# First batch of an attention and two-layer kernel: one pair of heads gets its own query and key buffers, six attention units move ahead in the planner's list, two move back

## Chip, cores and metric

The kernel runs on one core of one Trainium2 chip. The metric is the device time of one execution in microseconds, the median of the runs shown.

## What is computed

The reference, cut to what matters here: attention over 4 batches of 8 heads (576 positions, head size 64), where the first four heads see the last 32 positions and the other four see positions at multiples of 32, then two layers over the 2304 tokens.

```python
scores = scale * np.matmul(q, k.transpose(0, 1, 3, 2))
mask_local = (rel >= 0) & (rel < stride)
mask_strided = (rel >= 0) & (pos[None, :] % stride == pos[:, None] % stride)
scores = np.where(masks[None, :, :, :], scores, -1000000000.0)
scores = scores - np.max(scores, axis=-1, keepdims=True)
attn = np.exp(scores)
attn = attn / (np.sum(attn, axis=-1, keepdims=True) + 1e-09)
x = np.matmul(attn, v)            # per token: 8 heads x 64 = 512 values
h = np.maximum(np.maximum(x @ w1, x @ w2), x @ w3)     # 512 -> 768
x = h @ w_out                                          # 768 -> 512
h = x @ w_in                                           # 512 -> 2048
g = np.maximum(h, 0.0) + alpha * np.minimum(h, 0.0)
out = g @ w_out                                        # 2048 -> 512
```

All of it is float32. Dense products are made of three matmuls each, on a high and a low part of both factors (the pairs high-high, high-low, low-high).

## The kernel before

**The front of the kernel is list-scheduled.** The class `Weave` holds tasks: engines that may run one, a cost, a function that emits its instructions, a place in a list (`pos`), the events that it needs and gives, and the ring buffers that it takes and uses. When the program is built, `plan` goes through them: of all tasks whose needs are met and whose buffers will come free, it lets each engine take what can start first. Among tasks of an engine that can start within 120 ns of the earliest, the smallest `pos` goes first. A task off PE that reads a PSUM bank gets `pos - 1000`, so banks are emptied first. Buffers of the rings "q", "v", "e", "pt", "x" and "word" are handed out in the order in which the tasks were added. Each engine then runs its instructions in the order so planned.

**Attention.** Each batch has eight units, taken in the order of `ATT_UNITS`: heads in four pairs `cc`, two parts `hf` each. `(2, 0), (2, 1), (3, 0), (3, 1)` are the strided pairs, `(0, 0), (1, 0), (0, 1), (1, 1)` the local ones, whose `hf` is the half of the tokens. So the first six units of a batch give all that the first half of its tokens needs, and units seven and eight complete the second half. A unit is: scores on PE (L317), mask and row minimum on DVE (L325), exponentials on ACT (L332), reciprocals (L343, L344) and normalisation on DVE or ACT (L356, L354), transposes on PE (L367), copies of these to SBUF (L256), products with the values on PE (L392), then a high part of the output by a cast (L256) and a low part by a subtraction (L259). Two units of batch 0 have filler matmuls ahead of their first or second transposes (`UNREAD`, L362: three in unit three, nine in unit six), whose results nobody reads.

The tasks of batch 0 have `first, last = -32, -8` and `step = 2.4`: unit i (from 0) stands at -32 + 2.4 i, its transposes 2.4 later, its values 4.8 later. A pair's loads (L287 and L289 for queries and keys, L294 for values, all issued by SP) stand 8 places ahead of its first unit. Queries and keys have two buffers each (`qkp`), values two, exponentials three.

**Weights of the first layer.** 24 tiles (18 "gate", 6 "mix") come as float64 words: SP loads one (L437, three buffers `raw`), ACT rebases it (L451), DVE joins its words (L455, L457), ACT or DVE makes the high part (L256), DVE the low part (L259). Tile n stands at 1.5 n - 12 in the list, its load 4.5 earlier.

**Dense products.** One product of the first layer (L580, 12 matmuls of 128x288) needs one gate tile and the four pairs' outputs of one half of the tokens. They stand in the list from 0 on, in the order of `GATES_FIRST`: output features 0 and 1 of the first half, then feature 0 of the second half, then alternating. Three weights make one feature, of which the maximum is taken (L667, L670). L602 is the layer's second product. Attention of batch 1 stands from place 16 on, and its tasks run between the dense products.

**Later weights.** From place 44 on, the second layer's weights are converted as well and written to DRAM from three store tiles (`wst`, L489). What follows the list (the last batch's products, then the second layer, L986 to L1185) is written in a fixed order.

```python
weave = Weave({"bank": 8, "q": 2, "v": 2, "e": 3, "pt": 4, "x": 11, "t": 4, "h": 12,
               "raw": 3, "word": 6, "wst": 3})
...
add(load(592), emit_qk, pos, gives=[qk], makes=[("q", qk)])
...
first, last = (-32, -8) if b == 0 else ((b - 1) * NUNITS + (16 if b == 1 else 3), b * NUNITS - 3)
step = (last - first) / (len(ATT_UNITS) + 2)
...
attention_tasks(b, cc, hf, first + step * i, step)
```

## Time and profile before

| | us |
|---|---|
| median of 3 runs | 751.76 |
| lowest and highest run | 750.66, 752.38 |
| profiled execution, first to last instruction (span) | 747.7 |
| PE busy in it | 732.9 |
| PE weight loads (PEld) busy | 710.3 |
| DVE busy | 640.3 |
| ACT busy | 464.5 |

The profile gives the span of the profiled execution and not its device time; the device times are those of the runs, whose median lies 4.1 us above the span. "Idle before" in a row is the time in which the engine stood still just ahead of an instruction, with what ended it. PE is matmuls, PEld the weight loads, which run beside them. Matmuls are pipelined, so the rows of successive groups overlap a little. SPq is the queue of SP, from which all transfers here are issued. [...]

### The profile page before, as it was taken

What the parts mean: (1) busy time and instruction counts of PE and PEld (TensorE: products, weight loads), DVE (VectorE), ACT (ScalarE), POOL (GpSimd) and SP (SyncE); (2) the same over time, 40 slices, a digit from 0 to 9 for tenths busy, and PEclk for the clock granted to TensorE, in tenths of its full rate; (3) what the DMA queues carried; (4) which work ended last, traced back from release to release, by engine and by line L of the source; (5) the groups of instructions that cost most, each with busy time, mean ns of one, the idle gap of its engine ahead of it and who ended that gap; (6) DMA issues with size and microseconds to landing.
All of it is one profiled execution on the core that took longest, in us unless ns stands there. A gap on an engine that the chain in (4) does not pass through costs nothing.

```text
span 747.7 us, 16003 instructions
## 1 busy us (share of the span) xinstructions
PE 732.9 (98%) x5560; PEld 710.3 (95%) x5560; DVE 640.3 (86%) x1711; ACT 464.5 (62%) x1254; POOL 28.7 (4%) x42
## 2 busy tenths in 40 slices
PE   5899999999999999999999999999999999999998
PEld 4699999999999999999999999999999999999997
DVE  4899999899898999478868898888989888988896
ACT  5987889568684788423345666634666654556571
POOL 1000000000000000023500000000000000000000
PEclk9999999999999999999999999999999999999999
DMA  7477769996999765779899789999789999867362
GB/s 248 155 244 227 234 206 337 342 342 244 323 318 340 252 219 208 253 267 332 306 319 400 266 293 332 383 401 372 265 286 316 364 401 369 289 236 254 118 201 77
DMA packets 88929, 211.96 MB, mean 283 GB/s; under 512 B 11024, under 2 KB 41232, under 8 KB 88848
## 3 DMA queue, kind: packets, MB, share of 16 engines
q1 hardware_dynamic: 88848, 210.94, 80.4%
q8 instruction: 44, 0.72, 0.4%
q14 instruction: 37, 0.30, 0.1%
HBM read 154.80 MB, written 56.10 MB: 282 GB/s over the span
## 4 chain that ended last, share of the span: by engine, by line
PE 94%; ACT 2%; DMA 2%; DVE 1%; issue 0%; SPq 0%; ACTq 0%; DVEq 0%
PE bank L580 24%; PE ph L1185 23%; PE po L986 15%; PE bank L602 10%; PE bank L753 4%; PE po L992 4%; PE ph L986 3%; PE bank L317 3%; PE bank L392 2%; PE bank L367 2%; PE po L996 2%; ACT e L332 1%; DMA wh<-w 1%; DMA k<-in_kTs 0%; PE po L1185 0%; DMA wo<-w 0%
## 5 line engine op out<-in xcount | busy, mean ns | idle before, releaser
L1185 PE MATMUL ph<-x,w 128*128 128x384 f32 x990 | 200.1, 337 | 0.0
L580 PE MATMUL bank<-x,w 128*128 128x288 f32 x1440 | 197.5, 296 | 0.0
L580 PEld LDWEIGHTS bank<-x,w 128*128 128x128 f32 x1440 | 191.8, 188 | 2.1
L1185 PEld LDWEIGHTS ph<-x,w 128*128 128x128 f32 x990 | 166.3, 188 | 1.0
L986 PE MATMUL po<-w,g 128*128 128x256 f32 x936 | 135.6, 281 | 0.0
L986 PEld LDWEIGHTS po<-w,g 128*128 128x128 f32 x936 | 130.1, 189 | 0.4
L1191 DVE TENSOR_TENSOR c<-ph,c 128x384 f32<-128x384 f32 x165 | 89.5, 555 | 30.5 <-PE ph L1185 27.4
L979 ACT CAST g<-c 128x384 fp32r<-128x384 f32 x93 | 47.0, 505 | 91.1 <-DVE c L1169 51.7
L602 PE MATMUL bank<-h,w 128*128 128x288 f32 x576 | 79.4, 297 | 0.0
L602 PEld LDWEIGHTS bank<-h,w 128*128 128x128 f32 x576 | 76.9, 188 | 0.9
L256 ACT CAST w<-word 128x512 fp32r<-128x512 f32 x100 | 58.0, 590 | 24.8 <-DMA wh<-w 7.9
L332 ACT ACTIVATE e<-e,nm 96x128 f32<-96x128 f32 (+2 forms) x176 | 68.1, 396 | 6.1 <-DVE nm L325 5.9
L259 DVE TENSOR_TENSOR w<-word,w 128x512 fp32r<-128x512 f32 x100 | 63.4, 642 | 9.2 <-ACT w L256 8.9
L1129 ACT ACTIVATE c<-c 128x384 f32<-128x384 f32 x96 | 50.5, 526 | 32.9 <-DVE c L1191 31.8
L1130 ACT ACTIVATE c<-c,nalpha 128x384 f32<-128x384 f32 x96 | 59.2, 617 | 3.1
L1134 DVE SCALAR_TENSOR_TENSOR c<-c 128x384 f32<-128x384 f32 x96 | 53.1, 553 | 6.1 <-ACT c L1130 6.1
L980 DVE TENSOR_TENSOR g<-c,g 128x384 fp32r<-128x384 f32 x96 | 53.0, 552 | 0.9 <-ACT g L979 0.5
L451 ACT ACTIVATE word<-raw 128x512 f32<-128x512 f32 x56 | 37.6, 682 | 14.6 <-DMA raw<-in_w 10.8
L980 DVE TENSOR_TENSOR g<-k,g 128x384 fp32r<-128x384 f32 x72 | 37.2, 558 | 7.5 <-ACT g L979 7.5
L992 PE MATMUL po<-w,g 128*128 128x512 f32 x120 | 43.0, 397 | 0.0
L457 DVE SCALAR_TENSOR_TENSOR word<-raw,word 128x512 uint32<-128x512 uint32 x56 | 38.8, 692 | 1.9
L1169 DVE TENSOR_TENSOR k<-c 128x384 f32<-128x384 f32 x72 | 37.9, 551 | 0.0
(107 smaller groups left out, 939.1 us busy)
## 6 DMA issues: line engine op xcount, KB each, us to landing
w<-wh SPq DMA_DIRECT2D x72, 512.0 KB, 5.3
raw<-in_w SPq DMA_DIRECT2D x50, 512.0 KB, 5.1
w<-wo SPq DMA_DIRECT2D x48, 512.0 KB, 5.8
w<-wp SPq DMA_DIRECT2D x36, 512.0 KB, 6.4
wh<-w SPq DMA_DIRECT2D x24, 512.0 KB, 5.0
xd<-xst SPq DMA_DIRECT2D x28, 384.0 KB, 3.2
x<-xd SPq DMA_DIRECT2D x28, 384.0 KB, 8.2
ws<-w SPq DMA_DIRECT2D x12, 512.0 KB, 5.4
```

The lines of the kernel that those rows point to most:

```text
L256: (nc.scalar.copy if e == "ACT" else nc.vector.tensor_copy)(out_, in_)
L259: nc.vector.tensor_tensor(out=out_, in0=x, in1=y, op=ALU.subtract)
L332: nc.scalar.activation(tl[ek][:nq, j, i, :nk], tl[ek][:nq, j, i, :nk], AF.Exp, bias=tl["nm", u][:nq, j, i:i + 1], scale=-1.0, accum_out=tl ...
L580: nc.tensor.matmul(acc, words["gate", f, g][:, wi, cc * P:(cc + 1) * P], xt[b, cc, hf][:, xi, :], start=n == 0, stop=n == 3 * NCC - 1)
L602: nc.tensor.matmul(acc, words["mix", f][:, wi, dc * P:(dc + 1) * P], st["h", hf, f][:, xi, :], start=n == 0, stop=n == 3 * NF1 - 1)
L980: return g, lambda: nc.vector.tensor_tensor(out=g[:, 1], in0=x, in1=g[:, 0].bitcast(F32), op=ALU.subtract)
L986: nc.tensor.matmul(bank[:, NH * half:NH * (half + 1)], g[:, gi, t * P:(t + 1) * P], w[:, wi, off:off + NH], start=first and i == 0, stop=l ...
L992: nc.tensor.matmul(bank.rearrange("p (s n) -> p s n", n=NH), g[:, 0, t * P:(t + 1) * P], w[:, :, off:off + NH], start=first, stop=last)
L1130: nc.scalar.activation(a, a, AF.Copy, scale=nalpha[:, f:f + 1])
L1134: nc.vector.scalar_tensor_tensor(out=a, in0=h, scalar=0.0, in1=a, op0=ALU.max, op1=ALU.add)
L1185: nc.tensor.matmul(bank, words["h", n, i][:, wi, off + c * P:off + (c + 1) * P], x2h[blk, k, c][:, xi, :], start=m == 0, stop=m == 5)
L1191: nc.vector.tensor_tensor(out=out_, in0=bank, in1=other, op=ALU.add)
```

## The change

The third pair of heads of batch 0 (`cc = 0`, units five and seven) takes its queries and keys from a pool of its own, which lies in memory where the store tiles come later; the store tiles' pool is opened when the first of them is asked for, after the front pool is closed. In the list, units one to six of batch 0 move 200 places ahead, with transposes 0.3 and values 0.6 places behind their unit's first tasks; units seven and eight move ten places back (from -17.6 and -15.2 to -7.6 and -5.2), with the same 0.3. The places of all loads, of the weights, of the dense products and of the other batches stay.

```diff
+FRONT_POS, FRONT_STEP = -200, 0.3
...
-    qkp = pool(ax, "qkp", 2)
+    qk_pool = pool(ax, "qkp", 2)
...
-    wst = pool(conv_x, "wst", 3, "right")
+    front_x = ExitStack()
+    front_qk = pool(front_x, "fqk", 1, "right")
...
-    weave = Weave({"bank": 8, "q": 2, "v": 2, "e": 3, "pt": 4, "x": 11, "t": 4, "h": 12,
+    weave = Weave({"bank": 8, "q": 2, "third q": 1, "v": 2, "e": 3, "pt": 4, "x": 11, "t": 4, "h": 12,
                    "raw": 3, "word": 6, "wst": 3})
...
+        third = (b, cc) == (0, 0)
+
         def emit_qk(_):
+            qkp = front_qk if third else qk_pool
             q = qkp.tile([P, S], F32, tag="q", name="q")
...
-        add(load(592), emit_qk, pos, gives=[qk], makes=[("q", qk)])
+        add(load(592), emit_qk, pos, gives=[qk], makes=[("third q" if third else "q", qk)])
...
+    stores = []
+
+    def store_tile():
+
+        if not stores:
+            front_x.close()
+            stores.append(pool(conv_x, "wst", 3, "right"))
+        return stores[0].tile([P, 2, DM], F32R, tag="w", name="w")
...
-                    lambda: wst.tile([P, 2, DM], F32R, tag="w", name="w"), pos,
+                    store_tile, pos,
                     makes=[("wst", sk)], given=given)
...
-            attention_tasks(b, cc, hf, first + step * i, step)
+            attention_tasks(b, cc, hf, first + step * i + (FRONT_POS if i < 6 else 10) * (b == 0),
+                            step if b else FRONT_STEP)
```

## Rows read from the trace of the kernel before

**Rows 1.** The page's first part: busy us (share of span), instructions.

```profile
PE 732.9 (98%) x5560; PEld 710.3 (95%) x5560; DVE 640.3 (86%) x1711; ACT 464.5 (62%) x1254; POOL 28.7 (4%) x42
```

**Rows 2.** Busy us by stretch: us, length, engines, granted clock, DMA share, GB/s.

```profile
20.00:40.00 20.00, 17.41 (x187) 13.59 (x188) 18.09 (x103) 20.00 (x88) 0.00 (x0) 1.00 0.55 174
40.00:60.00 20.00, 20.00 (x153) 19.96 (x152) 19.36 (x43) 16.73 (x49) 0.00 (x0) 1.00 0.74 238
```

**Rows 3.** PE's waits: total us, times, longest; second row is from 38 to 300 us.

```profile
PE bank L317 <- DMA k<-in_kTs: 5.9, 2, 4.5
...
PE bank L317 <- ACT pt L256: 0.3, 1, 0.3
```

**Rows 4.** PE's timeline, 16 to 71 us: start, us, line, tiles, count, idle before.

```profile
16.50 1.32 PE L317 MATMUL bank<-k,q 64*96 64x128 f32 x12
...
20.70 0.90 PE L317 MATMUL bank<-k,q 64*96 64x128 f32 x12
...
26.20 0.72 PE L392 MATMUL bank<-pt,v 128*64 128x96 f32 x12 [0.41 <-ACT pt L256]
26.84 2.34 PE L362 MATMUL bank<-ident_r 128*128 128x512 f32 x9
29.79 1.00 PE L367 MATMUL bank<-ident,e 96*128 96x96 f32 x6 [0.61 <-DVE e L356]
...
33.11 0.71 PE L367 MATMUL bank<-ident,e 96*128 96x96 f32 x6
...
35.39 0.47 PE L367 MATMUL bank<-ident,e 96*128 96x96 f32 x3
...
36.81 0.82 PE L317 MATMUL bank<-k,q 64*108 64x108 f32 x12
37.56 0.95 PE L392 MATMUL bank<-pt,v 128*64 128x96 f32 x12
38.45 32.11 PE L580 MATMUL bank<-x,w 128*128 128x288 f32 x240
```

**Rows 5.** The timeline of ACT and DVE, 21 to 38 us.

```profile
21.87 1.23 ACT L451 ACTIVATE word<-raw 128x512 f32<-128x512 f32 x2
...
26.81 0.41 ACT L332 ACTIVATE e<-e,nm 96x128 f32<-96x128 f32 x1
...
28.56 0.16 DVE L343 TENSOR_SCALAR rc<-sm 96x6 f32<-96x6 f32 x1
...
30.43 0.38 DVE L455 TENSOR_SCALAR word<-word 128x512 uint32<-128x512 uint32 x1
...
30.84 0.69 DVE L457 SCALAR_TENSOR_TENSOR word<-raw,word 128x512 uint32<-128x512 uint32 x1
...
31.73 0.69 ACT L256 COPY pt<-bank 128x288 f32<-128x288 f32 x2
...
33.69 0.41 ACT L256 CAST x<-bank 128x288 fp32r<-128x288 f32 x1
...
34.14 0.46 DVE L259 TENSOR_TENSOR x<-bank,x 128x288 fp32r<-128x288 f32 x1 [0.70 <-ACT x L256]
...
36.70 0.68 DVE L259 TENSOR_TENSOR w<-word,w 128x512 fp32r<-128x512 f32 x1
```

**Rows 6.** Weight tiles finished on DVE, 0 to 72 us: ns min/median/max, first and last start.

```profile
L259 DVE TENSOR_TENSOR w<-word,w x15: 681/684/694, 36.7 to 71.7; 128x512 fp32r<-128x512 f32 x15
```

**Rows 7.** SP's queue, 7 to 15 us; key loads to landing; first and last store.

```profile
7.25 0.43 SPq L289 DMA_DIRECT2D k<-in_kTl  x1
7.72 1.38 SPq L437 DMA_DIRECT2D raw<-in_w  x3
14.70 0.43 SPq L289 DMA_DIRECT2D k<-in_kTl  x1
...
k<-in_kTl SPq DMA_DIRECT2D x8, 304.0 KB, 4.9
...
L489 SPq DMA_DIRECT2D wh<-w x32: 319/382/1348, 105.6 to 198.5; - x32
```

## The prediction

> **What bounds the kernel now.** I read the page's busy shares first. PE is busy 732.9 of 747.7 us [rows 1], so the only time to be won is time in which PE idles or waits. The table by stretches says where that is: in 20 to 40 us PE is busy 17.41 of 20.00 and its weight loads only 13.59, from 40 us on both are full [rows 2]. The list of PE's waits says the same: 5.9 us for the first key loads, and from 38 us to 300 us a single wait of 0.3 us [rows 3]. So everything hangs on when the stream of dense products begins, and on how much PE work is then already done. PE's timeline gives that start: 38.45 us, 240 matmuls in a row without a gap [rows 4].

> What ended last before it is read from the chain of waits and the rows of ACT and DVE. ACT is busy 20.00 of 20.00 in 20 to 40 us [rows 2]: it is the bound of the front. The first dense product (first half of the tokens, first weight) needs the attention output of the first six units of batch 0 and one finished weight tile. The sixth unit's output is finished by the subtraction at 34.14, thus at 34.60; the first weight tile by the subtraction at 36.70, thus at 37.38; then PE still has scores of batch 1 (36.81) and the eighth unit's values (37.56) ahead of it in its queue [rows 4, 5]. Units seven and eight, which this product doesn't need, sit in between: their twelve exponentials begin at 26.81 and hold the copies of the sixth unit's transposes back to 31.73, though those transposes start at 29.79 [rows 4, 5].

> **The change, part by part.** Four edits, told as three.

> *Own buffers for the third pair.* Its query and key loads no longer wait for the first pair's buffers; before the keys were issued at 7.25. A key load lands 4.9 us after its issue (median), so about 12.2, and the unit's scores run at 16.50: 4 us of slack. The fourth pair's keys, issued at 14.70, now take the first pair's buffers; they landed by about 19.6 and their scores run at 20.70, behind other PE work: 1 us of slack [rows 4, 7]. What really holds these scores is the ring of three exponential buffers, which is not touched. Behind them in SP's queue the first three weight loads move: past one more pair of some 0.6 MB, about 3 us at the pace at which weight tiles of 512 KB come later (2.5 us each). They were issued from 7.72, so their data would be there by about 21 instead of 18, as three follow each other; the first is read at 21.87 and joined at 30.43 [rows 5 to 7]. Bounds: nothing gained, 1 us lost if that cover went; taken: 0, since the first reader is nearest to the first of the three. The store tiles, made only once the front's buffers are closed, are first sent at 105.6, long after the last score of batch 0: 0 [rows 7].

> *First six units ahead, transposes and values right behind their unit (0.3 places instead of 2.4).* These units already stood ahead of the weights, and an instruction that empties a bank goes first anyway. So I expect the first 26 us as before, 0 from the order alone, within 1 us either way (the size of the waits in this stretch, PE idle before the sixth unit's transposes 0.61) [rows 4].

> *Units seven and eight ten places later.* The three weight tiles of the first output feature (places -12, -10.5, -9) now stand ahead of them (-7.6, -5.2), and so does the sixth unit's tail. On ACT the twelve exponentials from 26.81 to 31.73 (4.9 us) leave the path, as do the mask steps on DVE that push the sixth unit's reciprocal to 28.56 [rows 5]. What is late next: the nine filler matmuls ahead of the sixth unit's first transposes, from 26.84 for 2.34 us, to 29.18 [rows 4]. Transposes then start at 29.2 (before 29.79), are done about 30.0; the copies take 0.69 for two, 30.7; the values 0.72, 31.4; the cast 0.41 and the subtraction 0.46, **32.3**. The weight tile: joined on DVE at 30.43 before, in 1.1 us, and finished at 37.38 because its subtraction waited until 36.70. With the weights ahead, join 1.1, cast and subtraction (0.68, as much taken for the cast) follow each other: 30.4 + 2.4 = 32.8 at the latest, about 31 if the join moves ahead with the reciprocal [rows 5]. So the dense stream starts at about **32.5**, 5.95 us earlier. Bounds: 32.0 (nothing but the fillers and the tail) and 38.45 (as before).

> Against that, PE's work that stood between 33 and 38.45 must still be done inside the stream: transposes of units seven and eight 0.71 + 2 x 0.47, their values 2 x 0.72 (the row at 26.20; that at 37.56 includes waiting), two groups of scores of batch 1, 0.82 each at most. That is 4.73, less some 0.07 overlap at each of seven seams (36.81 + 0.82 ends after 37.56): **4.2 us** [rows 4]. Net -5.95 + 4.2 = -1.75. After that PE must not starve. A weight tile is finished every 2.5 us (fifteen from 36.7 to 71.7) and feeds one product of 12 matmuls, 1.6 us (32.11 / 20), while only the first half of the tokens is there, 3.2 us once both are [rows 4, 6]. The gap of 0.9 us per tile is covered by the 4.2 us of pushed-back work for four to five tiles, some 11 us. Taken: no idle.

> [...]

> **Sum.** On the profiled execution: 747.7 - 1.75 = 745.95 of span. The median of the runs is 4.1 above that span (751.76 - 747.7), kept as it is: 751.76 - 1.75 = **750.0 us**. About 0.2%, 1.5 us, is what a measurement of this kernel can tell from no change, so the forecast lies just beyond it.

> **Rivals.**

> A larger gain. If the planner also fills PE's remaining holes before the start (the 0.61 before the transposes, the stretched value rows, most of the 2.34 of fillers), 2 to 3 us more go: 747.5. For it: PEld only 13.59 of 20.00 [rows 2]. Against: ACT is full all through. 0.12.

> No gain: the list is only a preference. Each engine takes what can start first, so the idle PE may run units seven and eight's scores where it did, their mask steps go ahead as bank-emptiers, and the dense stream starts where the weights allow. A start at 36.5 would win 1.95 and pay about 2 back: 751.6. For it: the first weight tile was as late as the attention [rows 5]. 0.20.

> Slower: the second half comes too late. Now the weights stand ahead of units seven and eight on ACT and DVE, both full [rows 2]. Place: the dense stream after 32.5. Price: 0.9 us of PE idle per tile that serves only one half, less the 4.2 us of filling work and the gain of 1.75. It turns into a loss where the second half is later than 5.95 / 0.9 = 6.6 tiles (about 49 us); at eight tiles, 52.5 us, it is 7.2 - 4.2 - 1.75 = +1.25, at nine +2.15: 753.0 to 753.9, taken at 753.5. For it: DVE needs 2.5 us per tile with little else to do [rows 6]. Against: only the first three tiles outrank unit seven, the fourth and fifth unit eight. 0.20 (with later waits of a newly ordered list in it).

> The clock falls. If PE is slow again at the start of the stream, matmuls cost 1.32 / 0.90 there. The trace has PE slow from the first scores (4.5) to past 16.50, 12 us at most [rows 3, 4]; in a full stream I take half, 6 us, of which 1 - 0.90 / 1.32 = 0.32 is lost: -1.75 + 1.9 = 751.9, the loss bounded by 0 and 3.8. [...] 0.06.

> **How the numbers follow.** The forecast keeps 0.42, of which 0.08 falls short of 1.5 us. Faster: 0.34 + 0.12 = 0.46. Same: 0.08 + 0.20 + 0.06 = 0.34. Slower: 0.20. The forecast's own range is 748.9 to 751.0 (start at 32.0 to 33.5). The range for eight in ten takes in most of the larger gain and of the loss: 746.8 to 753.9.

> **What would show it.** Right: the first dense matmul between 32 and 33.5, with fewer than 240 matmuls in its first unbroken run; the transposes, values and batch 1's scores inside it; the copies of the sixth unit's transposes directly behind them; PE waits after the start below 0.5 us. Wrong: the first dense matmul past 36; PE waits on weight subtractions or on the second half's outputs after it; dense matmuls spaced above 0.134 us in the first microseconds; new waits past 100 us.

## The result, and the profile after

The changed kernel takes **759.49 us** (median; 758.33 to 763.68 in four runs) against 751.22 for the kernel before on the same chip: ratio 1.0122 as estimated from the runs (it is not the quotient of the medians), 95% interval 1.0097 to 1.0147. It is 8.3 us slower, where 750.0 was forecast and 753.9 was the upper end of the range. Lines of the code moved by two to fifteen: scores are now L322, masks L330, exponentials L337, reciprocals L348 and L349, normalisation L361 and L359, fillers L367, transposes L372, values L397, copies and casts L258, subtractions L261, weight joins L460 and L462, dense products L594. In the variants below they can lie some lines further on.

The profiled execution has a span of 756.5 us, 8.8 more than before. PE's busy time grew by 4.6 us although it runs the same 5560 matmuls [rows 1]; so it also ran slower:

```profile
PE 737.5 (97%) x5560; PEld 714.8 (94%) x5560; DVE 639.9 (85%) x1707; ACT 465.1 (61%) x1255; POOL 28.4 (4%) x42
```

In the list of PE's waits (total us, times, longest) the first of these lines stood at 1.9 us in the kernel before, and the other two are new [rows 3]:

```profile
PE bank L372 <- DVE e L361: 4.8, 2, 2.5
PE bank L594 <- ACT w L258: 3.3, 1, 3.3
PE ph L1200 <- ACT xo L823: 0.9, 1, 0.9
```

PE's timeline shows where they lie (start, us, shape and count, idle before with its releaser) [rows 4]:

```profile
19.52 0.90 PE L322 MATMUL bank<-k,q 64*96 64x128 f32 x12
20.35 0.78 PE L397 MATMUL bank<-pt,v 108*64 108x108 f32 x12
23.67 1.99 PE L372 MATMUL bank<-ident,e 126*126 126x126 f32 x10 [2.55 <-DVE e L361]
...
29.32 3.11 PE L367 MATMUL bank<-ident_r 128*128 128x512 f32 x9
...
32.62 0.90 PE L322 MATMUL bank<-k,q 64*96 64x128 f32 x12
...
38.66 6.37 PE L594 MATMUL bank<-x,w 128*128 128x288 f32 x24 [3.35 <-ACT w L258]
...
53.23 25.43 PE L594 MATMUL bank<-x,w 128*128 128x288 f32 x190 [0.56 <-DVE w L261]
78.50 1.15 PE L372 MATMUL bank<-ident,e 108*108 108x108 f32 x10
...
343.03 33.76 PE L767 MATMUL bank<-x,w 128*128 128x288 f32 x252
...
397.87 1.33 PE L1200 MATMUL ph<-x,w 128*128 128x384 f32 x6 [0.92 <-ACT xo L823]
```

Four things are to be seen. The sixth unit's scores come 1.2 us earlier than before (19.52, before 20.70). PE then stands still for 2.55 us ahead of the fourth unit's transposes. The nine fillers take 3.11 us instead of 2.34. And the dense stream starts at 38.66, no earlier than before, after another pause of 3.35 us, with 24 matmuls in 6.37 us: 0.265 us each, against 0.134 in the stream of before. Batch 1's first transposes, after 240 dense matmuls, stand at 78.50; before, the same point was 38.45 + 32.11, about 70.4. I use it below as the **checkpoint**: 8.1 us of the loss are there already. The last two rows are the longest dense run of the first layer (343.03; before it began at 335.28, so 7.75 us of the 8.8 are left there) and the start of the second layer, where 0.92 us of waiting are new.

The slow matmuls go with a lower granted clock of TensorE, the column ahead of the last two in the table by stretches (its second column is PE's busy time); in the kernel before it reads 1.00 over the whole span (0 to 748 us) [rows 2]:

```profile
22.00:24.00 2.00, 0.33 (x2) 0.23 (x3) 1.93 (x11) 2.00 (x12) 0.00 (x0) 1.00 0.00 0
24.00:26.00 2.00, 2.00 (x13) 1.51 (x14) 1.88 (x6) 2.00 (x8) 0.00 (x0) 0.55 0.00 0
26.00:28.00 2.00, 2.00 (x20) 1.56 (x16) 1.10 (x4) 1.63 (x6) 0.00 (x0) 0.50 0.14 34
...
36.00:38.00 2.00, 0.00 (x0) 0.00 (x0) 1.97 (x10) 2.00 (x12) 0.00 (x0) 0.96 0.33 126
38.00:40.00 2.00, 1.30 (x4) 0.95 (x5) 1.93 (x5) 2.00 (x9) 0.00 (x0) 0.50 0.69 205
```

Behind the first pause the clock reads 0.55 and then 0.50, and PE is busy for 2.00 of 2.00 us in each of these stretches. Behind the second it reads 0.50 from 38 to 44 us, where the 24 matmuls take their 0.265 us each.

What made the first pause is read from DVE's timeline (the first row is the end of the fourth unit's exponentials on ACT):

```profile
17.94 0.19 ACT L337 ACTIVATION_READ_ACCUMULATOR e<-e,nm 126x1 f32 x1
...
19.63 0.50 DVE L258 COPY pt<-bank 108x324 f32<-108x324 f32 x1 [1.06 <-PE bank L372]
...
20.85 0.28 DVE L330 CUSTOM_DVE_ANT_0 e<-bank,mask_l 96x128 f32<-96x128 f32 x1
...
22.59 0.16 DVE L348 TENSOR_SCALAR rc<-sm 126x4 f32<-126x4 f32 x1
...
23.15 1.64 DVE L361 TENSOR_TENSOR e<-e,rc 126x252 f32<-126x252 f32 x4
...
33.55 0.29 DVE L330 CUSTOM_DVE_ANT_0 e<-bank,mask_l 96x128 f32<-96x128 f32 x1 [3.22 <-PE bank L322]
...
36.32 0.42 DVE L460 TENSOR_SCALAR word<-word 128x512 uint32<-128x512 uint32 x1
```

and from the same rows of the kernel before:

```profile
20.15 0.16 DVE L343 TENSOR_SCALAR rc<-sm 126x4 f32<-126x4 f32 x1
...
20.55 0.75 DVE L356 TENSOR_TENSOR e<-e,rc 126x252 f32<-126x252 f32 x2
...
22.00 0.25 DVE L325 CUSTOM_DVE_ANT_0 e<-bank,mask_l 96x128 f32<-96x128 f32 x1
```

Before, the fourth unit's reciprocal (20.15) and normalisation (20.55) were done when the sixth unit's masks began (22.00). Now the six masks begin at 20.85 and stand **ahead** of that reciprocal (22.59) and normalisation (23.15), for which PE waits. The masks read PSUM banks, so the planner puts them 1000 places ahead of what empties no bank. They are not the whole of the delay: the fourth unit's exponentials were done by 18.13, and ahead of its reciprocal stood also 1.06 us in which DVE waited for PE's transposes, a copy, subtractions, and the last masks of the fifth unit. The six masks, from 20.85 to about 22.11, are 1.3 us of the 2.44 by which the reciprocal came later than before.

The second pause has its cause further down the same queue. ACT had rebased the weight words by 27.7, but DVE joins them only at 36.32: ahead of the joins stand the masks of the eighth unit (33.55, after 3.22 us of waiting for PE) and of batch 1's first unit. The eighth unit's scores (32.62) stand in PE's queue behind the nine fillers (29.32) and the first of the sixth unit's transposes.

### The profile page after: what moved, and what is told of

It is laid out like the page before. It is cut to its first block, busy times and chain, and to the rows that moved or that the text cites. A ratio compares the mean times of both kernels' runs of the same rounds, so it can differ in the third digit from the quotient of the medians.

```text
span 756.5 us, 16005 instructions
## 1 busy us (share of the span) xinstructions
PE 737.5 (97%) x5560; PEld 714.8 (94%) x5560; DVE 639.9 (85%) x1707; ACT 465.1 (61%) x1255; POOL 28.4 (4%) x42
## 4 chain that ended last, share of the span: by engine, by line
PE 74%; DVE 9%; DMA 8%; issue 3%; ACT 3%; POOL 2%; SPq 1%; POOLq 0%; ACTq 0%; DVEq 0%
PE ph L1200 23%; PE bank L594 16%; PE po L1001 15%; PE bank L616 6%; PE po L1007 4%; PE ph L1001 3%; DMA wh<-w 2%; PE bank L322 2%; PE po L1011 2%; PE bank L397 2%; PE bank L372 2%; ACT e L337 1%; DVE w L261 1%; POOL xst L215 1%; DVE e L330 1%
## 5 line engine op out<-in xcount | busy, mean ns | idle before, releaser
L594 PE MATMUL bank<-x,w 128*128 128x288 f32 x1440 | 201.8, 299 | 4.2 <-ACT w L258 3.3
L594 PEld LDWEIGHTS bank<-x,w 128*128 128x128 f32 x1440 | 194.6, 191 | 7.1 <-ACT w L258 3.5
L258 ACT CAST w<-word 128x512 fp32r<-128x512 f32 x100 | 57.6, 587 | 26.1 <-DMA wh<-w 11.5
L337 ACT ACTIVATE e<-e,nm 96x128 f32<-96x128 f32 (+2 forms) x176 | 67.8, 392 | 9.2 <-DVE nm L330 9.1
L261 DVE TENSOR_TENSOR w<-word,w 128x512 fp32r<-128x512 f32 x100 | 62.7, 640 | 9.8 <-ACT w L258 9.6
L462 DVE SCALAR_TENSOR_TENSOR word<-raw,word 128x512 uint32<-128x512 uint32 x56 | 38.8, 692 | 1.9
```

What stands on the lines that cost most here:

```text
L258: (nc.scalar.copy if e == "ACT" else nc.vector.tensor_copy)(out_, in_)
L261: nc.vector.tensor_tensor(out=out_, in0=x, in1=y, op=ALU.subtract)
L337: nc.scalar.activation(tl[ek][:nq, j, i, :nk], tl[ek][:nq, j, i, :nk], AF.Exp, bias=tl["nm", u][:nq, j, i:i + 1], scale=-1.0, accum_out=tl ...
L594: nc.tensor.matmul(acc, words["gate", f, g][:, wi, cc * P:(cc + 1) * P], xt[b, cc, hf][:, xi, :], start=n == 0, stop=n == 3 * NCC - 1)
```

## The experiments

"Clock" is the granted clock, "checkpoint" the start of batch 1's first transposes where 240 dense matmuls stand ahead of it as in the kernel before. A dash marks another order. Each ratio is to the kernel before on the same chip (medians there 750.66 to 751.22).

| variant | median us | ratio to before (95%) | longest PE pause at 21 to 28 | first dense | checkpoint |
|---|---|---|---|---|---|
| before | 751.22 | | 0.41 | 38.45 | 70.4 |
| changed | 759.49 | 1.0122 (1.0097, 1.0147) | 2.55 | 38.66 | 78.50 |
| bufs_alone | 750.95 | 0.9995 (0.9978, 1.0012) | 0.41 | 38.48 | 70.47 |
| list_alone | 752.74 | 1.0028 (1.0010, 1.0046) | 2.02 | 33.46 | 71.21 |
| old_step | 751.68 | 1.0026 (1.0006, 1.0045) | 0.41 | 32.95 | - |
| no_plus10 | 756.67 | 1.0085 (1.0068, 1.0102) | 2.55 | 43.20 | 75.41 |
| no_nine | 758.19 | 1.0093 (1.0066, 1.0120) | 2.55 | 35.16 | 75.07 |
| nine_at_fourth | 755.33 | 1.0068 (1.0052, 1.0083) | 0.19 | 34.35 | 72.98 |
| nine_at_both | 758.74 | 1.0092 (1.0063, 1.0120) | 0.19 | 36.17 | 75.71 |
| bridge | 756.60 | 1.0076 (1.0059, 1.0093) | 0.19 | 34.49 | 72.20 |
| calm_sixth | 751.72 | 1.0007 (0.9996, 1.0018) | 0.97 | 33.56 | 71.97 |
| reordered | 761.57 | 1.0154 (1.0119, 1.0188) | 1.67 | 40.44 | 80.08 |
| late_fourth | 758.00 | 1.0091 (1.0065, 1.0117) | 1.99 | 41.80 | 73.71 |
| nine_and_calm | 752.81 | 1.0028 (1.0015, 1.0040) | 0.17 | 30.80 | - |
| old_step_calm | 762.76 | 1.0158 (1.0131, 1.0184) | 0.41 | 36.35 | - |
| calm_sixth_eighth_b1 | 756.15 | 1.0091 (1.0054, 1.0127) | 0.97 | 31.81 | - |
| calm_sixth_b1 | 762.03 | 1.0145 (1.0119, 1.0171) | 0.97 | 33.89 | - |

### Which of the edits

**bufs_alone** keeps the own buffers and takes the list back.

```diff
-            attention_tasks(b, cc, hf, first + step * i + (FRONT_POS if i < 6 else 10) * (b == 0),
-                            step if b else FRONT_STEP)
+            attention_tasks(b, cc, hf, first + step * i,
+                            step)
```

> Edit: the own query and key buffers of the third pair alone, with the units at their old places and the old step in the list. Theory (the buffers cost and gain nothing by themselves, they only let the list's new places take effect): TensorE has no pause over 1 us up to 60 us, the first dense matmul is within 0.5 us of the 38.45 us of the kernel before, median 750.2 to 751.5. Rival (the earlier loads of the third pair push the first weights back, which costs): first dense matmul later by over 0.5 us, 752 or more.

Measured 750.95, no change, with the front of the kernel before. The buffers by themselves cost nothing.

**list_alone** is the opposite: the list without own buffers.

```diff
-        third = (b, cc) == (0, 0)
+        third = False
```

> The changed kernel without the third pair's own buffers: queries and keys share two buffers again, the list stays changed. Theory A (the buffers let scores, mask steps and normalisations pile up in another order, PE pauses 2.55 us at 21.1 and the granted clock falls): no pause over 1 us between 18 and 30 us, granted clock 1.00 in 24 to 32 us, first dense matmul 33 to 36, time 750 to 753. Theory B (the list places are at fault, whatever the buffers): pause and half clock as in the changed kernel, 757 to 760.

Measured +0.28% (interval 0.10 to 0.46). PE's timeline has a pause of nearly the same length, after which the clock read 0.50 in 24 to 26 us, and yet the dense stream starts five microseconds earlier than before:

```profile
23.18 1.22 PE L372 MATMUL bank<-ident,e 126*126 126x126 f32 x4 [2.02 <-ACT e L359]
...
27.74 0.90 PE L322 MATMUL bank<-k,q 64*96 64x128 f32 x12
...
33.46 2.27 PE L594 MATMUL bank<-x,w 128*128 128x288 f32 x14
```

So a pause need not be dear. Neither expectation holds as a whole: the time and the first dense matmul are theory A's, the pause and the low clock theory B's. The pause is also not the one of the changed kernel. DVE and ACT show it:

```profile
19.33 0.16 DVE L348 TENSOR_SCALAR rc<-sm 126x4 f32<-126x4 f32 x1
...
22.72 0.70 ACT L359 ACTIVATE e<-e,rc 126x126 f32<-126x126 f32 x2
```

Here the fourth unit's reciprocal (19.33) runs ahead of the sixth unit's masks (whose scores begin at 19.56), and it is the normalisation, left to ACT behind the fifth unit's exponentials, that comes late. What differs further is what stands behind the pause: the eighth unit's scores (27.74) come ahead of fillers and sixth transposes, and DVE never stands still for them.

**old_step** takes the transposes' distance back to 2.4 places, and keeps all else.

```diff
-                            step if b else FRONT_STEP)
+                            step)
```

> The changed kernel with transposes 2.4 and values 4.8 places behind their unit, as before, instead of 0.3 and 0.6. If the depth-first order makes the pause at 21.1 (theory C): transposes of the fourth and fifth unit apart again, granted clock 1.00 in 24 to 32 us, 750 to 753. If the buffers alone make it (theory A): pause and clock as in the changed kernel, 757 to 760.

Measured +0.26% (0.06 to 0.45): the pause at 21 us is gone, the clock is 1.00 in every stretch from 18 to 48 us, the dense stream begins at 32.95, and then, after two matmuls, waits 1.50 us for the low part of its tile. Theory C holds. With the two runs before, nearly all of the loss needs both: own buffers **and** the short distance.

**no_plus10** leaves units seven and eight where they were.

```diff
-            attention_tasks(b, cc, hf, first + step * i + (FRONT_POS if i < 6 else 10) * (b == 0),
+            attention_tasks(b, cc, hf, first + step * i + (FRONT_POS if i < 6 else 0) * (b == 0),
```

> The changed kernel with units seven and eight at their old places (-17.6, -15.2). If the places of these units make the loss (theory D): 750 to 753, clock 1.00. By theories A and C the pause at 21 us comes before these units play a part: the granted clock still falls to 0.5 after it, the first dense matmul waits for both units as in the kernel before and begins past 40 us at half clock or shortly after it; 756 to 760.

Measured 756.67: the first pause is unchanged (2.55 us), a second of 2.34 us ends at 35.7, and the first dense matmul comes at 43.20, as theories A and C have it. The ten places are not what makes the pause.

### What the fillers and the clock take

Three variants move the nine fillers, which stand ahead of the sixth unit's first transposes: away (**no_nine**), into the pause ahead of the fourth unit's transposes (**nine_at_fourth**), or to both (**nine_at_both**).

```diff
-UNREAD = {((0, 3, 0), 1): 3, ((0, 1, 0), 0): 9}
+UNREAD = {((0, 3, 0), 1): 3}
...
+UNREAD = {((0, 3, 0), 1): 3, ((0, 3, 1), 0): 9}
...
+UNREAD = {((0, 3, 0), 1): 3, ((0, 3, 1), 0): 9, ((0, 1, 0), 0): 9}
```

> The changed kernel without the nine filler matmuls ahead of the sixth unit's first transposes; every other instruction keeps its place. Clock falls as before after the pause at 21.1 us (0.5 in 24 to 30). If the fillers' place costs about what they last (3.1 us at half clock): sixth unit's transposes near 29.3, first dense matmul 35 to 36 behind the same late weight tile, 755 to 757. If the clock alone matters and the fillers keep it up later: no gain or a loss, 759 or more.

> The changed kernel with the nine filler matmuls ahead of the fourth unit's first transposes, into the pause at 21.1 us, instead of ahead of the sixth unit's. Clock theory (the pause lowers the clock, and that and the fillers at half clock cost most of the 8 us): granted clock 1.00 in 22 to 34 us, the sixth unit's transposes about 3 us earlier, first dense matmul 33 to 36, at full clock if PE doesn't pause long before it; 751 to 754. Rival (the weight tiles joined late on DVE set the start whatever the clock does): first dense matmul still past 37, 756 to 759.

> The changed kernel with nine fillers more, ahead of the fourth unit's first transposes (in PE's pause), those of the sixth unit kept; every other instruction keeps its place. It adds PE work and only keeps the clock up. Clock theory: 1.00 from 22 to 35 us, sixth unit's transposes at about 30 instead of 32.3, first dense matmul 36 to 37, 756 to 758: faster than the changed kernel although it does more. Rival (more work on a full front): 759.5 or more.

The front went about as first expected in all three; each median (758.19, 755.33, 758.74) lies above the range of that expectation and below its rival's. With the changed kernel the three make a square at the checkpoint. With no fillers in the pause, the nine ahead of the sixth's transposes cost 78.50 - 75.07 = 3.4 us; with the clock kept up, 75.71 - 72.98 = 2.7. Fillers in the pause gain 78.50 - 75.71 = 2.8 and 75.07 - 72.98 = 2.1: they bring the fourth unit's transposes no earlier (23.70 and 23.83, in the changed kernel 23.67), but the clock reads 1.00 up to 34 us, where it was 0.50 to 0.74 from 24 to 32 us in the changed kernel. The fillers filled a gap before [rows 4]; behind the pause they lie on the path. What is left in nine_at_fourth is the late weight tile, with the clock down again behind it (0.54 in 34 to 36 us, 0.61 in 36 to 38):

```profile
34.35 5.05 PE L594 MATMUL bank<-x,w 128*128 128x288 f32 x24 [3.74 <-ACT w L258]
```

At the end the medians of no_nine and nine_at_both have only 1.3 and 0.75 us left of the 3.4 and 2.8 that they had won at the checkpoint, and their intervals overlap that of the changed kernel, so no gain at the end is shown. Their traces have waits further on (no_nine: 1.1 us for one of the maxima, 1.5 at the start of the second layer; nine_at_both: 3.1 there).

**bridge** is nine_at_fourth with 14 more fillers in that wait, in the bank of the dense product itself.

```diff
+        full = bank()
+        for _ in range(14 if (b, hf, f, g) == (0, 0, 0, 0) else 0):
+            nc.tensor.matmul(full.rearrange("p (r n) -> p r n", n=P), ident_r,
+                             ident_r.unsqueeze(1).to_broadcast([P, 4, P]), start=True, stop=True)
+        acc = full[:, :HALF]
```

> Edit: the variant with nine fillers at the fourth unit (755.33 us), and 14 more filler matmuls ahead of the first dense product, written into that product's own bank before it, to fill the 3.74 us for which TensorE waits there for its weights. Theory (a part of the loss is that the dense product then runs its first 24 matmuls at half clock: 5.05 us, against about 3.2 at full clock): the granted clock stays over 0.9 in 34 to 38 us, the first 24 take 3.2 to 3.5 us, and the median is 753.0 to 754.0. Rival (the tile's lateness alone is the loss, and the speed of the first matmuls is made good by later waits for the next tiles): the first 24 are quick, a wait for the second or third tile takes their place, and the median is 755.0 to 755.7.

```profile
30.67 3.47 PE L592 MATMUL bank<-ident_r 128*128 128x512 f32 x14
34.49 0.53 PE L598 MATMUL bank<-x,w 128*128 128x288 f32 x2 [0.35 <-ACT w L258]
35.22 3.29 PE L598 MATMUL bank<-x,w 128*128 128x288 f32 x22 [0.20 <-DVE w L261]
...
72.20 1.15 PE L372 MATMUL bank<-ident,e 108*108 108x108 f32 x10
```

The 24 matmuls are through in 4.0 us, a wait of 0.20 included, instead of 5.05, and the checkpoint comes 0.78 us earlier: the first theory in kind, though not in size. The median, 756.6, was foreseen by neither, and the intervals don't tell it from the 755.33 of nine_at_fourth: PE waits 2.8 us at the start of the second layer (1.7 in nine_at_fourth), and the clock reads 0.91 in 380 to 400 us (1.00 in nine_at_fourth). Up to the checkpoint, though, the account closes: with PE's other work in the order of the changed kernel, the nine fillers moved into the first pause and 14 put into the second, 78.50 becomes 72.20, within 0.25 us of the next variant, in which the pauses are not filled but shrink or go. The medians of these two are 4.9 us apart all the same: the checkpoint does not settle the end.

### The order on DVE

**calm_sixth** takes the rank of bank-emptiers from the sixth unit's masks alone (`URGENT` is the 1000).

```diff
+        calm = Weave.URGENT if u in ((0, 1, 0),) else 0
...
-            add((dve(nk, 2),), masked, pos, needs=[("sc", u)], gives=[("nm", u, i)],
+            add((dve(nk, 2),), masked, pos + calm, needs=[("sc", u)], gives=[("nm", u, i)],
```

> Edit: of the changed kernel only the sixth unit's masks (third pair, first half) lose the planner's rank of bank-emptiers, so that VectorE takes the fourth unit's reciprocal and normalisation ahead of four of the six. Theory (TensorE's 2.55 us pause at 21.1 us comes from those six masks standing ahead of the fourth unit's normalisation, and the granted clock of 0.50 in 24 to 30 us comes from the pause): the fourth unit's transposes start near 21.3 instead of 23.67, the wait ahead of them is under 1 us, the granted clock stays at 1.00 up to the end of the sixth unit's transposes, and batch 1's first transposes start 2 to 3 us ahead of the changed kernel's 78.50; median 755.5 to 757.5. Rival (the pause is set by ScalarE's exps of the fourth unit, or by the order of the list itself): the wait stays over 2 us and the clock falls as before; 758 to 760. If the pause goes and the clock falls nonetheless, the clock has another cause.

**751.72 us, the time of the kernel before** (ratio 0.9996 to 1.0018): the theory's way, and 4 us further than it had it. The pause is down to 0.97, and the clock, 0.55 in this stretch of the changed kernel, is 1.00 here and in every stretch up to 46 us:

```profile
22.43 0.62 PE L373 MATMUL bank<-ident,e 126*126 126x126 f32 x4 [0.97 <-DVE e L362]
...
27.59 2.34 PE L368 MATMUL bank<-ident_r 128*128 128x512 f32 x9
30.77 1.14 PE L373 MATMUL bank<-ident,e 96*128 96x96 f32 x6 [0.84 <-ACT e L360]
...
33.56 2.31 PE L595 MATMUL bank<-x,w 128*128 128x288 f32 x14
36.05 3.21 PE L595 MATMUL bank<-x,w 128*128 128x288 f32 x22 [0.18 <-DVE w L261]
...
47.69 24.44 PE L595 MATMUL bank<-x,w 128*128 128x288 f32 x180
71.97 1.15 PE L373 MATMUL bank<-ident,e 108*108 108x108 f32 x10
```

```profile
24.00:26.00 2.00, 1.93 (x17) 1.21 (x18) 1.47 (x10) 2.00 (x10) 0.00 (x0) 1.00 0.10 23
```

The fillers are back in a gap (0.84 us of waiting still follows them), and the dense stream starts at 33.56 with the clock at 1.00. The caution: the planner made another list from it, in which PE's order differs too (the eighth unit's scores come at 25.81, ahead of fillers and sixth transposes). The two runs that follow were to separate this.

**reordered** keeps the planned list, PE's and ACT's orders included, and changes only when DVE's instructions are emitted: the fourth unit's reciprocal and normalisation, a subtraction, and the fifth unit's reciprocal and normalisation go ahead of four of the six masks. In DVE's order:

```diff
+L348 TENSOR_SCALAR rc<-sm 126x2x2
+L349 RECIPROCAL rc<-rc 126x2x2
+L361 TENSOR_TENSOR e<-e,rc 126x2x126 x2
+L261 TENSOR_TENSOR x<-bank,x 128x9x18 x2
+L348 TENSOR_SCALAR rc<-sm 96x6
+L349 RECIPROCAL rc<-rc 96x6
+L361 TENSOR_TENSOR e<-e,rc 96x384 x2
 L330 ISA e,nm<-bank,mask_l 96x128
...
-L261 TENSOR_TENSOR x<-bank,x 128x9x18 x2
-L348 TENSOR_SCALAR rc<-sm 126x2x2
-L349 RECIPROCAL rc<-rc 126x2x2
-L348 TENSOR_SCALAR rc<-sm 96x6
-L349 RECIPROCAL rc<-rc 96x6
-L361 TENSOR_TENSOR e<-e,rc 126x2x126 x2
-L361 TENSOR_TENSOR e<-e,rc 96x384 x2
```

> Edit: the changed kernel with its planned list left as it is, TensorE's and ScalarE's instructions in the same order; on VectorE alone the fourth unit's reciprocal and normalisation, the subtraction of the fifth's and the fifth unit's reciprocal and normalisation go ahead of four of the sixth unit's six masks. Theory (VectorE's order makes the pause, the pause the low clock, and the rest of the loss, the fillers and late weight tiles, stands in TensorE's own order, which is kept): the waits ahead of the fourth and the fifth unit's transposes are under 1.4 us each, the granted clock stays over 0.9 in 20 to 32 us, the sixth unit's transposes start near 29.5 us instead of 32.3, the wait for the first weight tile is still over 2 us, median 754.0 to 756.5. First rival (VectorE's order is the whole cause): also the first dense matmul starts before 34 us at full clock, median 751.0 to 753.0. Second rival (TensorE's order is the whole cause): clock and pause mend, but the end does not, 757.5 to 760.

761.57, no faster than the changed kernel (the intervals overlap); all three expectations missed, because the edit didn't remove the wait but cut it in three:

```profile
23.21 0.74 PE L402 MATMUL bank<-ident,e 126*126 126x126 f32 x4 [1.12 <-DVE e L387]
24.90 0.84 PE L402 MATMUL bank<-ident,e 96*128 96x96 f32 x6 [0.95 <-DVE e L387]
27.41 1.37 PE L428 MATMUL bank<-pt,v 126*64 126x126 f32 x8 [1.67 <-ACT pt L259]
```

The last of the three is new: the sixth unit's exponentials now wait for their masks, and the copies of the fourth unit's transposes stand behind them on ACT. PE is idle for 3.74 us in sum, none longer than 1.67, and the clock falls all the same (0.90 in 24 to 26, 0.50 from 26 to 32 us). With the changed kernel's order on PE and ACT, this swap on DVE alone mends nothing.

**late_fourth** makes the pause in the order of before: bufs_alone with 12 needless additions ahead of the fourth unit's reciprocal.

```diff
             rc, sm = tl["rc", u], tl["sm", u]
+            for _ in range(12 if u == (0, 3, 1) else 0):
+                nc.vector.tensor_scalar_add(rc[:nq, :, :n], sm[:nq, :, :n], 1e-9)
```

> Edit: the variant with own buffers alone (750.95 us, in its front the order of the kernel before), and the fourth unit's addition ahead of the reciprocal written 13 times instead of once, some 2.2 us of needless work on VectorE at the place where the changed kernel has the sixth unit's masks. Theory (a pause there costs through the clock wherever the weight tiles stand): TensorE waits 1.8 to 2.6 us ahead of the fourth unit's transposes, the granted clock falls under 0.7 after it, the first dense matmul starts 2 to 4 us after the 38.5 of that variant, median 753 to 755. Rival (in the order of before the pause falls into slack, since four waits of 0.6 to 2.2 us and nine fillers follow it): the first dense matmul within 1 us of 38.5, median 750.7 to 752; then the changed kernel loses not by the pause but by what its order puts behind it.

```profile
24.61 0.73 PE L374 MATMUL bank<-ident,e 126*126 126x126 f32 x4 [1.99 <-DVE e L363]
...
41.80 32.07 PE L596 MATMUL bank<-x,w 128*128 128x288 f32 x240
73.71 1.15 PE L374 MATMUL bank<-ident,e 108*108 108x108 f32 x10
...
394.82 3.91 PE L1202 MATMUL ph<-x,w 128*128 128x384 f32 x12 [3.17 <-ACT xo L825]
```

The pause is 1.99 us, the clock 0.58 and 0.57 in the four microseconds from 26 on, and the dense stream starts 3.3 us late (41.80 against 38.48): the theory's size. The end is 7 us late, twice that. The rest is the last row: at the start of the second layer PE waits 3.17 us, and its next 12 matmuls take 3.91 us, where twelve of this form behind them take 2.24. The theory's median, 753 to 755, is missed by that. Twelve additions, 2.4 us of work on DVE, cost 7 us.

### Towards something faster

Four variants take the masks' rank away elsewhere too, so that the joins of the first weight tiles come earlier: **nine_and_calm** (with the fillers at the fourth unit) and **old_step_calm** (with the old distance) for units seven, eight and batch 1's first, **calm_sixth_eighth_b1** and **calm_sixth_b1** for the units in their names. All are the edit of calm_sixth with another tuple of units:

```diff
+        calm = Weave.URGENT if u in ((0, 0, 1), (0, 1, 1), (1, 2, 0)) else 0
...
+        calm = Weave.URGENT if u in ((0, 1, 0), (0, 1, 1), (1, 2, 0)) else 0
...
+        calm = Weave.URGENT if u in ((0, 1, 0), (1, 2, 0)) else 0
```

> The changed kernel with the fillers at the fourth unit, and with the mask steps of units seven and eight and of batch 1's first unit at their own places in the list instead of 1000 ahead, so that the first weight tiles are joined ahead of them on DVE. If the two causes (clock, late weight tile) make the whole loss: no PE pause over 1 us between 18 us and the first dense matmul, that one at 30 to 32.5, clock 1.00; 748 to 751.5. If a third cause is left (the second half too late): PE waits for it past 35 us, 752 or more.

> The changed kernel with transposes and values 2.4 and 4.8 places behind their unit, as before, and the mask steps of units seven and eight and of batch 1's first unit at their own places, fillers as they were. The plain version with 2.4 waited 1.5 us for the first weight tile and 1.3 us for a normalisation left to ACT. If the late tile is what keeps it from gaining: first dense matmul 31 to 33.5 with no wait for a weight, 748.5 to 750.5. If tiles joined earlier only delay units seven and eight: PE waits after 35 us, 751 to 753.

> Edit: of the changed kernel the masks of the sixth and the eighth unit and of batch 1's first unit lose the rank of bank-emptiers, so that VectorE takes the fourth unit's normalisation, and later the joins of the first weight tiles, ahead of them. Theory (both of TensorE's pauses, 2.55 us at 21.1 and 3.35 us ahead of the dense product, come from masks that stand ahead on VectorE): both are under 1 us, the granted clock is over 0.9 all through 20 to 40 us, the first dense matmul starts before 34 us, and the median is 751.5 to 754.0; what is left against the kernel before is the nine fillers on the path and the second half's later tiles. Rival (masks that come later only move the wait to the eighth unit's values or to batch 1's first transposes, as in the variant with the old step and later masks): a wait of over 3 us at the eighth unit's values or transposes between 35 and 60 us, the clock falls there, 757 to 763.

> Edit: of the changed kernel the masks of the sixth unit and of batch 1's first unit lose the rank of bank-emptiers. Theory (with the first pause gone the early dense product still loses some 1.9 us by waits for its next weight tiles, whose joins stand behind masks; batch 1's masks can come later): the first 60 dense matmuls take under 9.0 us in sum instead of 9.55, batch 1's first transposes start before 71.9 us, median 750.2 to 751.5. Rival (batch 1's first unit is then late, as the second half was in the variant with three units' masks later): a wait of over 1 us ahead of batch 1's transposes or values, median 752 to 754.

The tiles do come earlier: the dense stream starts at 30.80 in nine_and_calm and at 31.81 in calm_sixth_eighth_b1. But then units seven and eight are late, and PE runs dry inside the stream. PE's rows of calm_sixth_b1:

```profile
43.13 1.83 PE L595 MATMUL bank<-x,w 128*128 128x288 f32 x12
49.98 1.53 PE L398 MATMUL bank<-pt,v 128*64 128x96 f32 x12 [5.01 <-ACT pt L258]
51.43 27.62 PE L595 MATMUL bank<-x,w 128*128 128x288 f32 x192
```

That is the second half coming too late: 5.01 us here, 6.72 in old_step_calm ahead of values too, 1.97 and 2.51 ahead of transposes in calm_sixth_eighth_b1, which lies between its two expectations. Nine_and_calm went its rival's way (752.81, and a wait of 2.23 us ahead of transposes); old_step_calm and calm_sixth_b1 did too, and much further. None of them beats the kernel before; the nearest are bufs_alone and calm_sixth, which equal it.

## Why the prediction was wrong

**The step that failed** is "first six units ahead": "the first 26 us as before, 0 from the order alone, within 1 us either way". It looked at the places that moved and not at who is now ready at the same time. In these 26 us PE now stands still for 2.55 us, and 6.5 us at the checkpoint hang on it. The shorter distance brings the sixth unit's scores 1.2 us forward (19.52; 19.56 in list_alone, which has no own buffers; 20.11 in old_step, which has the old distance). With the own buffers added, their masks then come ahead of the fourth unit's reciprocal, since a bank-emptier wins; without them the reciprocal still came first (list_alone). Why the buffers turn this order round was not traced. The sentence "an instruction that empties a bank goes first anyway" named the rule and drew the wrong conclusion from it.

**What it set off**, by the runs: in the order of before such a pause costs 3.2 us at the checkpoint (late_fourth, 73.71 - 70.47). In the order of the changed kernel 6.5 us hang on it (78.50 against calm_sixth's 71.97, PE's other order there included), and two things stand behind it: the fillers come onto the path (2.7 to 3.4 us, a share of the 6.5), and the eighth unit's scores behind them hold up DVE's joins, so that PE pauses again. With the 1.5 us by which calm_sixth itself stands behind bufs_alone, these are about the 8.1 us of the checkpoint, of which 7.75 are left at 343.03; with the wait of 0.92 at the second layer's start that is nearly all of the 8.8 us of span.

**The clock.** I gave it 0.06 and put it at the start of the dense stream. It did fall, and that stream did start at half speed (granted clock 0.50 from 38 to 44 us, 0.265 us a matmul against 0.134); but both times behind a pause, of 2.55 and of 3.35 us. The factor 1.32 / 0.90 that I put on it did not go with a lower granted clock: in the kernel before, that reads 1.00 in 16 to 18 us too, where the 1.32 stands. In calm_sixth, with 3.9 us of transposes between 20 and 40 us among scores, values and fillers, it is 1.00 in every stretch from 20 to 46 us; no run here has transposes alone. What I left out is that the clock can fall behind a pause of PE, as it did here, and that the wait is then paid twice.

**Own buffers**: taken as 0, measured as 0 (bufs_alone), but only by themselves. In the changed list they make the difference between 752.74 (list_alone) and 759.49, which the sum of separate parts had no term for. The third pair's keys were issued at 4.02 instead of 7.25, the weight loads at 7.65, as before [rows 7].

**Units seven and eight later**: tested where nothing disturbs it, in calm_sixth. The start of the dense stream was put at 32.5 and is 33.56, inside the bounds; the tile (32.8 at the latest) was finished at 32.83, and the fillers hid nothing more. The tail was not right: the sixth unit's transposes start at 30.77 instead of 29.2, and its subtraction ends at 35.0 instead of 32.3:

```profile
34.57 0.45 DVE L261 TENSOR_TENSOR x<-bank,x 128x288 fp32r<-128x288 f32 x1
```

That the dense stream could begin at 33.56 all the same is luck: the product takes this pair of heads last. The work pushed into the stream was put at 4.2 us and takes 0.85 + 0.72 + 0.66 + 1.27 + 1.00 = 4.50. What failed here is "taken: no idle": the first 60 dense matmuls, in five pieces, take 9.55 us instead of 60 x 0.134 = 8.03, and PE waits 0.18 to 0.21 us ahead of three of the pieces; how the rest divides was not measured. The next 180 take 24.44 instead of 24.1. So the sum is -4.92 + 4.50 + 1.86 = +1.4 at the checkpoint (measured 71.97 - 70.47 = +1.5), not -1.75; at the end the medians differ by 0.7, which the interval doesn't tell from nothing. The gain of 1.75 wasn't there even without the pause.

**The rivals.** "The second half too late" had the right sign and the wrong cause for this kernel: after the dense start its waits are 0.56 and 0.3 us. In the four variants that finish the weights still earlier it is just what happened, though. "No gain, the masks go ahead as bank-emptiers" saw the mechanism and put it at units seven and eight, at the price of the gain.

**What stays open.** Why PE stalls at the start of the second layer: 3.17 us in late_fourth and none in bufs_alone, which issue the same instructions in the same order but for the 12 additions; 0.92 in the changed kernel, none in calm_sixth or before. PE waits for a copy of the last outputs of the first layer, and that copy for the landing of an earlier store (in late_fourth PE waits 3.2 us for the copy and ACT 2.4 us for the store; in bufs_alone ACT waits 1.8 us for the store and PE not for the copy); why the stores are late in one and not in the other wasn't tried. And PE's order and DVE's order could not be parted cleanly, as reordered made a wait of its own.

## What to carry to other kernels

When a list is reordered, ask of each engine's queue not only what has moved but which instructions are now ready at the same moment, and who waits for the one that loses: here six masks of 0.21 us each, 1.3 us of DVE work, came ahead of one normalisation, and with their rank taken away 7.8 us were back. A pause of the matmul engine was paid again in the clock here (2.55 us of it, then a granted clock of 0.50 to 0.55 from 24 to 30 us), and for what was hidden in an old gap (fillers, joins) ask anew what hides it now. Test the parts of a list edit singly and together: here the buffers alone cost nothing, the list alone 0.28%, both 1.2%.

## What was not expected of the hardware

```profile
38.57 0.89 PE L373 MATMUL bank<-ident,e 96*128 96x96 f32 x3 [1.97 <-ACT e L360]
...
398.33 1.33 PE L1200 MATMUL ph<-x,w 128*128 128x384 f32 x6 [3.11 <-ACT xo L823]
```

With nine filler matmuls, whose results nobody reads, in the pause of 2.55 us, it read 1.00 from 20 to 34 us (nine_at_fourth), and with 14 in the wait ahead of the dense stream that stream began at 1.00 (bridge, 34 to 36 us).
